# Attention with a position bias and a feed-forward layer: the mixed tile's scores, and the first unit's, straight from fp32 q and k

## The chip, the cores and the metric

The kernel runs on one core of one Trainium2 chip. A core has TensorE (PE in the profile; PEld is its weight load), VectorE (DVE), ScalarE (ACT), GpSimd (POOL), and SyncE (SP), which here issues every DMA. The metric is the device time of one execution in microseconds (us), the median of three runs.

## The reference

The kernel computes attention with a learned bias that depends on the distance of two positions, and then a feed-forward layer on the attention's output:

```
scores = q @ k.T / sqrt(64)                       # q, k, v: (4, 8, 576, 64)
psi_rel, psi_i = log1p(|i - j|), log1p(max(i, 1))
h = relu((psi_rel / psi_i)[..., None] @ w1 + b1)  # 32 hidden
scores += (h @ w2) per head                       # 8 heads
attn = softmax(scores);  a = attn @ v             # -> x: (2304, 512)
g = max(0.01 * y, y) with y = x @ w_in            # (512, 2048)
out = g @ w_out                                   # (2048, 512)
```

All inputs and outputs are fp32.

## The kernel before

There are three stages.

**The bias.** `gen_tick(g)` runs 36 times. A tick takes 16 rows of the bias for all heads: four relu tiles r of the hidden layer are made by DVE (L116) or ACT (L114), as a plan by costs decided; PE multiplies them with w2 (L127, four products of 32 output rows); ACT evicts the result into a tile e (L134, L135); SP writes e to a scratch array scr in DRAM (L146). From scr, `load_bias` (L163 to L172) reads the biases back, in the form that the scores want, as tiles "0", "1", "M", "2" and "3"; their loads are issued at ticks 16, 24, 27, 34 and 37.

**The attention.** It runs in 16 units u; a unit is a pair of heads and one batch entry. A unit has nine tiles in the order A0 B0 A1 B1 M A2 B2 A3 B3. A tile is 128 rows of scores by 576 columns; A tiles belong to the first head, B tiles to the second, and the mixed tile M holds the last 64 rows of both. `step(n)` handles tile n: `qk_mm` (scores, PE, L234), the reduction with bias (DVE, L258), then the transposes of tile n-3 (PE, L300 and L318), which ACT copies into PT (L316), then, where a group of tiles is complete, the product with v (PE, L335: 10 fp32 products of 64 output rows, each of which the profile shows as two records), then the exponential (ACT, L266). The scores' PSUM tile ps_s has two buffers, so the scores of tile n+2 wait for DVE's reduction of tile n. All is issued in a fixed order, written out by the program; each engine and SP's queue go through theirs in order.

The scores are made from two-part numbers: `split_hi` casts raw q (L196) and raw k (L201) to fp32r on DVE, `split_lo` takes the remainder on POOL (q L208, k L211). The tile qs has the high part of q in partitions 0 to 63 and the low part in 64 to 127; ks1 has k's high part, ks2 its low part, each in both halves. A tile of scores is then four products with all 128 partitions (two halves of 288 columns, with ks1 and with ks2). Tile M has eight, since the rows of the two heads need different k: the second half of the products is added onto the first, and a zero block of qs (set at L65) keeps each head's rows out of the other's.

The table SPL says at which tile i of unit u the splits of unit u+1 are issued. Those of unit 0 stand in the bias stage: from tick 6 on, every second tick issues one of `sp_ops` (q's cast, two q subtractions, k's cast, two k subtractions). `load_unit(u)` (L176 to L182) brings raw q and k of a unit into one of two pairs of tiles raw_b, each twice, once per partition half; units 0 and 1 are loaded at the start, unit u+2 after step i = 0 of unit u. `gen.close()` frees the bias stage's tiles at n = 8.

**The feed-forward layer.** It follows the last unit, with its own loads and products (L452, L478 to L480); the change does not touch it.

Of the kernel before, what the change touches and what calls it, by code (L numbers as in the profile page):

```python
# [8 lines left out]
F32 = mybir.dt.float32  # L9
F32R = mybir.dt.float32r  # L10
# [4 lines left out]
B, H, S, D, HID = 4, 8, 576, 64, 32  # L15
DM, DFF = 512, 2048
NT = B * S
HP = H // 2
KC = DM // 128
MF = DFF // 128  # L20
HS = S // 2
S0 = 512 - HS
PIT = S + 32
KW = 2 * S + 64
EARLY = 7
KINDS = ["A0", "B0", "A1", "B1", "M", "A2", "B2", "A3", "B3"]
GEN = [16, 17] + list(range(16)) + [34, 35] + list(range(18, 26)) + list(range(33, 25, -1))
SPL = {0: [(0, "q")], 1: [(1, "q", 0)], 3: [(1, "q", 1)], 4: [(0, "k")], 5: [(1, "k", 0)], 7: [(1, "k", 1)]}
GEN_AT = [39] * 9
LAG = 3  # L30
BLK = 512
# [5 lines left out]
def attention_ffn(ctx: ExitStack, tc: tile.TileContext, qt, kt, vm, vt, wi, wo, cst, out):  # L37
    nc = tc.nc
# [5 lines left out]
    gp = gen.enter_context(tc.tile_pool(name="gen", bufs=1, side="right"))  # L44
    att = ExitStack()
    ap = att.enter_context(tc.tile_pool(name="att", bufs=1, reuse_waits="tile"))
# [4 lines left out]
    def pstile(tag):  # L51
        shape = [128, 1024] if tag == "s" else [128, 512]
        return ps.tile(shape, F32, tag=tag, name="ps_" + tag)

    tmp_x = {(m, i): xp.tile([128, DM], F32, name=f"y{m}{i}") for m in range(5, EARLY) for i in range(2)}
    raw_b = [[ap.tile([128, c], F32, name=f"raw{c}{i}") for c in (2 * S, KW)] for i in range(2)]
# [3 lines left out]
    for t in vt_b:  # L60
        nc.vector.memset(t[0:64, 1, :], 0.0)
        nc.vector.memset(t[64:128, 0, :], 0.0)
    qs_b = [ap.tile([128, 1280], F32R, name=f"qs{i}") for i in range(2)]
    for t in qs_b:
        nc.vector.memset(t[:].rearrange("p (a c) -> p a c", a=2)[:, :, 576:640].bitcast(F32), 0.0)  # L65

    PT = ap.tile([128, 2, 10, HS], F32, name="PT")

    cs = gp.tile([128, S + 214], F32, name="cs")
    bps = gp.tile([128, 144], F32, name="bps")  # L70
    warm = gp.tile([128, 1], F32, name="warm")
# [19 lines left out]
    def gen_w(T):  # L91
        return max(S - 16 * T, 16 * T + 16)

    plan, load = [], {"a": 0.0, "v": 5.0}
    for T in GEN:
        w = gen_w(T)
# [77 lines left out]
    raw, qk, vv = {}, {}, {}  # L174

    def load_unit(u):  # L176
        hp, b = divmod(u, B)
        q_, k_ = raw_b[u % 2]
        for p in (0, 64):
            nc.sync.dma_start(out=q_[p:p + 64], in_=qt[hp, b])  # L180
            nc.sync.dma_start(out=k_[p:p + 64], in_=kt[hp, b])
        raw[u] = (q_, k_)  # L182

    def load_v(u):
# [7 lines left out]
    def split_hi(u, what):  # L192
        q_, k_ = raw[u]
        if what == "q":
            qs = qs_b[u % 2]
            nc.vector.tensor_copy(qs[:].rearrange("p (a c) -> p a c", a=2)[:, :, 0:S], q_[:].rearrange("p (a c) -> p a c", a=2))  # L196
            ks1 = ap.tile([128, KW], F32R, tag="ks1", name="ks1", bufs=2)
            ks2 = ap.tile([128, KW], F32R, tag="ks2", name="ks2", bufs=2)
            qk[u] = (qs, ks1, ks2)
        else:  # L200
            nc.vector.tensor_copy(qk[u][1][:], k_[:])  # L201

    def split_lo(u, what, a):
        q_, k_ = raw[u]
        qs, ks1, ks2 = qk[u]
        if what == "q":
            dst = qs[64:128, 640 * a:640 * a + S]
            nc.gpsimd.tensor_sub(dst, q_[64:128, S * a:S * a + S], dst.bitcast(F32))  # L208
        else:
            c = slice(S * a, KW if a else S)  # L210
            nc.gpsimd.tensor_sub(ks2[:, c], k_[:, c], ks1[:, c].bitcast(F32))  # L211

    st, pp = {}, {}

    def tile_id(n):
        u, i = divmod(n, 9)
        return u, KINDS[i]

    def qk_mm(n):
        u, kind = tile_id(n)  # L220
        qs, ks1, ks2 = qk[u]
        s_ = pstile("s")
        if kind == "M":
            prs = [(512, 0), (576, S + 64)]
        elif kind[0] == "A":
            prs = [(128 * int(kind[1]), 0)]
        else:
            prs = [(704 + 128 * int(kind[1]), S)]
        nmm = len(prs) * 2
        j = 0  # L230
        for c0, k0 in prs:
            for ks in (ks1, ks2):
                for hh in range(2):
                    nc.tensor.matmul(s_[:, S0 + HS * hh:S0 + HS * hh + HS], qs[:, c0:c0 + 128], ks[:, k0 + HS * hh:k0 + HS * hh + HS], start=(j == 0), stop=(j == nmm - 1))  # L234
                j += 1
        st[n] = s_

    mx_t, sm_t, rb_t, pair = {}, {}, {}, [None]
# [1 line left out]
    def softmax_a(n):  # L240
        u, kind = tile_id(n)
        hp = u // B
        bt = bias[hp, "M"][:] if kind == "M" else bias[hp, kind[1]][:, 0 if kind[0] == "A" else 1, :]
        col = 1 if kind[0] == "B" else 0
        if col == 0:
            mx_t[n] = ap.tile([128, 2], F32, tag="mx", name="mx", bufs=6)
        else:
            mx_t[n] = mx_t[n - 1]
        g, sc = int(KINDS.index(kind) > 4), 4 if kind == "M" else 2 * (int(kind[1]) % 2) + col
        if kind in ("A0", "A2"):  # L250
            sm_t[u, g] = ap.tile([128, 12], F32, tag="sm", name="sm", bufs=3)
        if kind == "M":
            pair[0] = ap.tile([128, S + 64], F32, tag="pM", name="pM", bufs=1)
        elif col == 0:
            pair[0] = ap.tile([128, 2 * S], F32, tag="p", name="p", bufs=3)
        p = pair[0][:, S * col:S * col + S]
        s_, i = st.pop(n), mx_t[n][:, col:col + 1]
        nc.vector.tensor_tensor_reduce(out=p, in0=s_[:, S0:S0 + S], in1=bt, scale=-0.125, scalar=3.4e38, op0=ALU.add, op1=ALU.min, accum_out=i)  # L258
        pp[n] = pair[0]
        ex_q.append((p, i, sm_t[u, g][:, sc:sc + 1]))  # L260
# [101 lines left out]
    def step(n):  # L362
        if n < NTILE:
            qk_mm(n)
            softmax_a(n)
        if 0 <= n - 1 < NTILE and KINDS[(n - 1) % 9] in ("M", "B3"):
            recip(n - 1)
        x_steps()
        while pv_out:
            pv_exit()  # L370
        if 0 <= n - LAG < NTILE:
            transposes(n - LAG, n + 2)
        if pv_q and pv_q[0][0] <= n:
            pv()
        while ex_q:
            softmax_b()
# [113 lines left out]
    with tc.manual_schedule():  # L490
        gen_setup()
        for u in range(2):
            load_unit(u)
            load_v(u)
        sp_ops = [(u, w, a) for u in range(1) for w, a in (("q", None), ("q", 0), ("q", 1), ("k", None), ("k", 0), ("k", 1))]
        done = -1
        early_ops = []
        for n in range(NTILE + LAG + 6):
            u, i = divmod(n, 9)
            if u == 0:  # L500
                while done < GEN_AT[i]:
                    gen_tick(done)
                    done += 1
                    if done >= 6 and done % 2 == 0 and sp_ops:
                        w = sp_ops.pop(0)
                        split_hi(*w[:2]) if w[2] is None else split_lo(*w)
            if n == 8:
                gen.close()
                early = ctx.enter_context(tc.tile_pool(name="early", bufs=1, side="right"))
                x_alloc(early, 0)  # L510
                w_alloc(early, 0)
                early.tile([128, 24], F32, name="gap")
                stage, stage_y = ExitStack(), ExitStack()
                pools["s"] = stage.enter_context(tc.tile_pool(name="stage", bufs=1, side="right"))
                pools["y"] = stage_y.enter_context(tc.tile_pool(name="stage_y", bufs=1, side="right"))
            step(n)
            if n == 13:
                w_fill()
                for m in range(EARLY):
                    early_ops += [(w_abs, m, h) for h in range(2)]  # L520
                    early_ops += [(w_bits, m, h, k) for k in range(4) for h in range(2)]
                    if m == 0:
                        early_ops += [(w_hi, 0, h) for h in range(2)] + [(w_lo, 0, h, nc.vector) for h in range(2)]
            for _ in range({0: 3, 4: 3}.get(i, 0) if n >= 18 else 0):
                if early_ops:
                    f, *args = early_ops.pop(0)
                    f(*args)
            if n == NTILE + 2:
                ffn1(0, 0)
            if u < HP * B:  # L530
                if u % B == B - 1 and u // B + 1 < HP:
                    c = {1: "0", 2: "1", 3: "M", 4: "2", 6: "3"}.get(i)
                    if c:
                        load_bias(u // B + 1, c)
                if u + 1 < HP * B:
                    for f, *args in SPL.get(i, ()):
                        (split_hi, split_lo)[f](u + 1, *args)
                if i == 0 and u + 2 < HP * B:
                    load_unit(u + 2)
                if i == 8 and u + 2 < HP * B:  # L540
                    load_v(u + 2)
        att.close()
# [35 lines left out]
        for j in range(len(seq) + 2):  # L578
            if j < len(seq):
                n, m = seq[j]  # L580
# [57 lines left out]
```

## Time and profile before

| | |
|---|---|
| three runs | 714.15, 712.75, 712.86 us; median 712.86 |
| the profiled execution | 713.1 us, its span 711.3 us |
| granted TensorE clock, mean | 0.999 |
| PE busy | 697.9 us, 98% of the span |
| DVE, ACT, POOL busy | 371.7, 362.6, 120.4 us |
| bias stage | from the start to about 56 us |
| attention | from about 56 us to about 315 us |
| feed-forward layer | from there to the end |

A row of the chain of waits gives the start, the time and the engine and line of one piece of the path that sets the end; a row of the timeline gives the records of one engine in order, with the idle time ahead of them in brackets. Records of products overlap (a weight load is done beside the product before it), so pieces of the chain, not record lengths, add up to time.

### The profile page before, as it was taken

How to read it: one execution, taken by the hardware profiler on the slowest of the kernel's cores; microseconds unless marked ns; L12 is line 12 of the kernel's file. 1: busy time of each engine (PE TensorE's matmuls, PEld its weight loads, DVE VectorE, ACT ScalarE, POOL GpSimd, SP SyncE). 2: the span in 40 equal slices, each digit the busy share in tenths (PEclk: the TensorE clock that was granted, in tenths of full speed). 3: DMA queues.
4: the chain of work that ended last, by engine and by line, in shares of the span. 5: the costliest groups of instructions: out<-in, count | busy, mean ns of one | idle time of the engine just before them, and what ended most of it. 6: DMA issues, size and time to landing. Idle time of an engine off the chain costs nothing.

```text
span 711.3 us, 11144 instructions
## 1 busy us (share of the span) xinstructions
PE 697.9 (98%) x4192; PEld 558.0 (78%) x4192; DVE 371.7 (52%) x876; ACT 362.6 (51%) x792; POOL 120.4 (17%) x143
## 2 busy tenths in 40 slices
PE   6899999999999999999999999999999999999997
PEld 2346888788888888877888888888888888888896
DVE  6996788878888878559995211122111221111111
ACT  7698778778787787684654221123111321222221
POOL 2203454445454444200000000000000000000000
PEclk9999999999999999999999999999999999999999
DMA  8798929755966772003550000001000010000100
GB/s 212 246 315 247 250 63 277 144 161 131 250 162 177 208 194 77 1 1 103 169 173 0 33 27 1 1 0 60 1 0 1 0 60 1 0 1 0 60 1 30
DMA packets 30262, 68.26 MB, mean 96 GB/s; under 512 B 8192, under 2 KB 8320, under 8 KB 30208
## 3 DMA queue, kind: packets, MB, share of 16 engines
q1 hardware_dynamic: 30208, 67.54, 33.7%
q8 instruction: 33, 0.54, 0.3%
q14 instruction: 21, 0.17, 0.1%
HBM read 51.92 MB, written 15.61 MB: 95 GB/s over the span
## 4 chain that ended last, share of the span: by engine, by line
PE 94%; DVE 3%; DMA 1%; issue 0%; ACT 0%; DVEq 0%; SPq 0%
PE ps_o L452 13%; PE ps_t L452 13%; PE ps_s L234 12%; PE ps_o L335 12%; PE ps_s L480 9%; PE ps_s L478 9%; PE ps_s L479 9%; PE ps_t L300 8%; PE ps_o L127 2%; PE ps_t L127 2%; DVE r L116 2%; PE ps_s L127 1%; PE ps_o L318 1%; PE ps_o L289 1%; DMA scr<-x 1%
## 5 line engine op out<-in xcount | busy, mean ns | idle before, releaser
L467 DVE TENSOR_TENSOR gl<-g,gh 128x512 fp32r<-128x512 f32 (+1 forms) x80 | 51.0, 638 | 266.2 <-ACT g L461 266.2
L234 PE MATMUL ps_s<-ks,qs 128*128 128x288 f32 x640 | 120.6, 315 | 1.5 <-DVE mx L258 1.5
L480 PE MATMUL ps_s<-woh,gl 128*128 128x512 f32 x288 | 112.1, 389 | 0.3 <-DVE gl L467 0.3
L478 PE MATMUL ps_s<-woh,gh 128*128 128x512 f32 x288 | 112.3, 390 | 0.0
L479 PE MATMUL ps_s<-wol,gh 128*128 128x512 f32 x288 | 112.2, 390 | 0.0
L258 DVE CUSTOM_DVE_ANT_0 p<-ps_s,bias 128x576 f32<-128x576 f32 x128 | 94.2, 750 | 26.0 <-PE ps_s L234 24.1
L234 PEld LDWEIGHTS ps_s<-ks,qs 128*128 128x128 f32 x640 | 89.7, 189 | 16.1 <-issue 8.2
L266 ACT ACTIVATE p<-p,mx 128x576 f32<-128x576 f32 x128 | 100.0, 781 | 3.7 <-DVE mx L258 3.0
L316 ACT COPY PT<-ps_t 128x512 f32<-128x512 f32 x128 | 73.9, 578 | 53.6 <-PE ps_t L300 53.6
L460 ACT ACTIVATE gh<-ps_o 128x512 fp32r<-128x512 f32 (+1 forms) x39 | 21.5, 552 | 126.6 <-PE ps_o L452 126.6
L460 ACT ACTIVATE gh<-ps_t 128x512 fp32r<-128x512 f32 (+1 forms) x39 | 21.5, 552 | 112.0 <-PE ps_t L452 111.9
L300 PE MATMUL ps_t<-ident,p 128*128 128x128 f32 x512 | 76.4, 272 | 0.0
L335 PE MATMUL ps_o<-PT,v 128*64 128x288 f32 x512 | 69.2, 412 | 0.0
L480 PEld LDWEIGHTS ps_s<-woh,gl 128*128 128x128 f32 x288 | 54.1, 188 | 12.1 <-DVE gl L467 0.7
L300 PEld LDWEIGHTS ps_t<-ident,p 128*128 128x128 f32 x512 | 62.4, 140 | 0.4 <-issue 0.4
L479 PEld LDWEIGHTS ps_s<-wol,gh 128*128 128x128 f32 x288 | 54.1, 188 | 10.7
L478 PEld LDWEIGHTS ps_s<-woh,gh 128*128 128x128 f32 x288 | 54.1, 188 | 10.6
L452 PE MATMUL ps_t<-xh,wil 128*128 128x512 f32 (+1 forms) x156 | 57.3, 367 | 0.0
L452 PE MATMUL ps_o<-xh,wil 128*128 128x512 f32 (+1 forms) x156 | 57.3, 367 | 0.0
L452 PE MATMUL ps_o<-xl,wih 128*128 128x512 f32 (+1 forms) x156 | 57.3, 367 | 0.0
L452 PE MATMUL ps_t<-xl,wih 128*128 128x512 f32 (+1 forms) x156 | 57.3, 367 | 0.0
L452 PE MATMUL ps_o<-xh,wih 128*128 128x512 f32 (+1 forms) x156 | 57.2, 367 | 0.0
(108 smaller groups left out, 1075.6 us busy)
## 6 DMA issues: line engine op xcount, KB each, us to landing
raw<-kt SPq DMA_DIRECT2D x32, 304.0 KB, 6.0
raw<-qt SPq DMA_DIRECT2D x32, 288.0 KB, 5.8
raw<-wi SPq DMA_DIRECT2D x16, 512.0 KB, 4.1
raw<-wo SPq DMA_DIRECT2D x16, 512.0 KB, 3.6
scr<-x SPq DMA_DIRECT2D x21, 295.5 KB, 4.2
bias<-scr SPq DMA_DIRECT2D x16, 288.0 KB, 5.4
out<-x SPq DMA_DIRECT2D x18, 256.0 KB, 2.1
v<-vm SPq DMA_DIRECT2D x16, 256.0 KB, 5.2
```

The lines of the kernel that those rows point to most:

```text
L234: nc.tensor.matmul(s_[:, S0 + HS * hh:S0 + HS * hh + HS], qs[:, c0:c0 + 128], ks[:, k0 + HS * hh:k0 + HS * hh + HS], start=(j == 0), stop= ...
L258: nc.vector.tensor_tensor_reduce(out=p, in0=s_[:, S0:S0 + S], in1=bt, scale=-0.125, scalar=3.4e38, op0=ALU.add, op1=ALU.min, accum_out=i)
L266: nc.scalar.activation(out=p, in_=p, func=AF.Exp, bias=i, scale=-1.0, accum_out=sm)
L300: nc.tensor.transpose(t0[:, 128 * jb:128 * jb + 128], p[:, p0 + 128 * jb:p0 + 128 * jb + 128], ident[:])
L316: nc.scalar.copy(out=PT[:, g, 0:8, c].rearrange("p (j h) c -> p j h c", h=2)[:, :, h, :], in_=t0[:].rearrange("p (j c) -> p j c", j=4))
L335: nc.tensor.matmul(o[64 * h:64 * h + 64, 0:HS], l, r, start=(jb == 0), stop=(jb == 4))
L452: nc.tensor.matmul(h_[:, :N], w, x[:, :N], start=(j == 0), stop=(j == len(mms) - 1))
L460: nc.scalar.activation(out=gh[:, :N], in_=h_[:, :N], func=AF.Prelu, alpha=0.01)
L467: nc.vector.tensor_sub(gl[:, :N], g[:, :N], gh[:, :N].bitcast(F32))
L478: nc.tensor.matmul(o, gh[:, c], wt[m][2][:], start=(m == 0), stop=False)
L479: nc.tensor.matmul(o, gh[:, c], wt[m][3][:], start=False, stop=False)
L480: nc.tensor.matmul(o, gl[:, c], wt[m][2][:], start=False, stop=(m == MF - 1))
```

## The change

Three things are done.

1. Tile M's scores are four fp32 products of one quadrant each: raw q and k of one partition half hh (partitions 64 hh to 64 hh + 63) give 288 columns of scores, in a PSUM bank of their own; head h goes to output rows 64 h to 64 h + 63. No part is added to another, so the zero blocks of qs and their memsets are gone, and qs has 1024 columns in place of 1280. Its cast is 1024 columns wide (1152 before), and each q subtraction 512 (576).
2. In unit 0 every tile reads raw fp32 q and k: two products per tile, one per partition half, each of 64 contracted rows and 288 columns. Unit 0 has no casts and no subtractions. Its raw tiles are its own (raw_0), in the bias stage's pool, which is now closed at n = 9.
3. Since tile M reads raw q and k, `load_unit(u+2)`, which overwrites them, is issued behind M's scores (i = 4), not after step i = 0; a unit's four raw loads go q, q, k, k. The q cast moves from i = 0 to i = 1 and q's first subtraction from i = 1 to i = 2; k's splits stay.

```diff
--- before.py
+++ after.py
@@ -25,7 +25,7 @@
 EARLY = 7
 KINDS = ["A0", "B0", "A1", "B1", "M", "A2", "B2", "A3", "B3"]
 GEN = [16, 17] + list(range(16)) + [34, 35] + list(range(18, 26)) + list(range(33, 25, -1))
-SPL = {0: [(0, "q")], 1: [(1, "q", 0)], 3: [(1, "q", 1)], 4: [(0, "k")], 5: [(1, "k", 0)], 7: [(1, "k", 1)]}
+SPL = {1: [(0, "q")], 2: [(1, "q", 0)], 3: [(1, "q", 1)], 4: [(0, "k")], 5: [(1, "k", 0)], 7: [(1, "k", 1)]}
 GEN_AT = [39] * 9
 LAG = 3
 BLK = 512
@@ -60,12 +60,11 @@
     for t in vt_b:
         nc.vector.memset(t[0:64, 1, :], 0.0)
         nc.vector.memset(t[64:128, 0, :], 0.0)
-    qs_b = [ap.tile([128, 1280], F32R, name=f"qs{i}") for i in range(2)]
-    for t in qs_b:
-        nc.vector.memset(t[:].rearrange("p (a c) -> p a c", a=2)[:, :, 576:640].bitcast(F32), 0.0)
+    qs_b = [ap.tile([128, 1024], F32R, name=f"qs{i}") for i in range(2)]
 
     PT = ap.tile([128, 2, 10, HS], F32, name="PT")
 
+    raw_0 = [gp.tile([128, c], F32, name=f"raw{c}") for c in (2 * S, KW)]
     cs = gp.tile([128, S + 214], F32, name="cs")
     bps = gp.tile([128, 144], F32, name="bps")
     warm = gp.tile([128, 1], F32, name="warm")
@@ -175,10 +174,10 @@
 
     def load_unit(u):
         hp, b = divmod(u, B)
-        q_, k_ = raw_b[u % 2]
-        for p in (0, 64):
-            nc.sync.dma_start(out=q_[p:p + 64], in_=qt[hp, b])
-            nc.sync.dma_start(out=k_[p:p + 64], in_=kt[hp, b])
+        q_, k_ = raw_b[u % 2] if u else raw_0
+        for t, src in ((q_, qt), (k_, kt)):
+            for p in (0, 64):
+                nc.sync.dma_start(out=t[p:p + 64], in_=src[hp, b])
         raw[u] = (q_, k_)
 
     def load_v(u):
@@ -193,7 +192,7 @@
         q_, k_ = raw[u]
         if what == "q":
             qs = qs_b[u % 2]
-            nc.vector.tensor_copy(qs[:].rearrange("p (a c) -> p a c", a=2)[:, :, 0:S], q_[:].rearrange("p (a c) -> p a c", a=2))
+            nc.vector.tensor_copy(qs[:].rearrange("p (a c) -> p a c", a=2), q_[:].rearrange("p (a c) -> p a c", a=2)[:, :, 64:S])
             ks1 = ap.tile([128, KW], F32R, tag="ks1", name="ks1", bufs=2)
             ks2 = ap.tile([128, KW], F32R, tag="ks2", name="ks2", bufs=2)
             qk[u] = (qs, ks1, ks2)
@@ -204,8 +203,8 @@
         q_, k_ = raw[u]
         qs, ks1, ks2 = qk[u]
         if what == "q":
-            dst = qs[64:128, 640 * a:640 * a + S]
-            nc.gpsimd.tensor_sub(dst, q_[64:128, S * a:S * a + S], dst.bitcast(F32))
+            dst = qs[64:128, 512 * a:512 * a + 512]
+            nc.gpsimd.tensor_sub(dst, q_[64:128, S * a + 64:S * a + S], dst.bitcast(F32))
         else:
             c = slice(S * a, KW if a else S)
             nc.gpsimd.tensor_sub(ks2[:, c], k_[:, c], ks1[:, c].bitcast(F32))
@@ -218,21 +217,29 @@
 
     def qk_mm(n):
         u, kind = tile_id(n)
+        s_ = pstile("s")
+        q_, k_ = raw[u]
+        if kind == "M":
+            for hh in range(2):
+                r = slice(64 * hh, 64 * hh + 64)
+                for h in range(2):
+                    k0 = (S + 64) * h + HS * hh
+                    nc.tensor.matmul(s_[64 * h:64 * h + 64, S0 + HS * hh:S0 + HS * hh + HS], q_[r, S * h:S * h + 64], k_[r, k0:k0 + HS], start=True, stop=True)
+            st[n] = s_
+            return
+        c0, k0, h = 128 * int(kind[1]), 0, 0
+        if kind[0] == "B":
+            c0, k0, h = c0 + 512, S, 1
+        if u == 0:
+            for hh in range(2):
+                r, c = slice(64 * hh, 64 * hh + 64), c0 + 64 + 64 * h
+                nc.tensor.matmul(s_[:, S0 + HS * hh:S0 + HS * hh + HS], q_[r, c:c + 128], k_[r, k0 + HS * hh:k0 + HS * hh + HS], start=True, stop=True)
+            st[n] = s_
+            return
         qs, ks1, ks2 = qk[u]
-        s_ = pstile("s")
-        if kind == "M":
-            prs = [(512, 0), (576, S + 64)]
-        elif kind[0] == "A":
-            prs = [(128 * int(kind[1]), 0)]
-        else:
-            prs = [(704 + 128 * int(kind[1]), S)]
-        nmm = len(prs) * 2
-        j = 0
-        for c0, k0 in prs:
-            for ks in (ks1, ks2):
-                for hh in range(2):
-                    nc.tensor.matmul(s_[:, S0 + HS * hh:S0 + HS * hh + HS], qs[:, c0:c0 + 128], ks[:, k0 + HS * hh:k0 + HS * hh + HS], start=(j == 0), stop=(j == nmm - 1))
-                j += 1
+        for j, ks in enumerate((ks1, ks2)):
+            for hh in range(2):
+                nc.tensor.matmul(s_[:, S0 + HS * hh:S0 + HS * hh + HS], qs[:, c0:c0 + 128], ks[:, k0 + HS * hh:k0 + HS * hh + HS], start=(j == 0), stop=(j == 1))
         st[n] = s_
 
     mx_t, sm_t, rb_t, pair = {}, {}, {}, [None]
@@ -362,6 +369,8 @@
     def step(n):
         if n < NTILE:
             qk_mm(n)
+            if n % 9 == 4 and n // 9 + 2 < HP * B:
+                load_unit(n // 9 + 2)
             softmax_a(n)
         if 0 <= n - 1 < NTILE and KINDS[(n - 1) % 9] in ("M", "B3"):
             recip(n - 1)
@@ -492,7 +501,6 @@
         for u in range(2):
             load_unit(u)
             load_v(u)
-        sp_ops = [(u, w, a) for u in range(1) for w, a in (("q", None), ("q", 0), ("q", 1), ("k", None), ("k", 0), ("k", 1))]
         done = -1
         early_ops = []
         for n in range(NTILE + LAG + 6):
@@ -501,10 +509,7 @@
                 while done < GEN_AT[i]:
                     gen_tick(done)
                     done += 1
-                    if done >= 6 and done % 2 == 0 and sp_ops:
-                        w = sp_ops.pop(0)
-                        split_hi(*w[:2]) if w[2] is None else split_lo(*w)
-            if n == 8:
+            if n == 9:
                 gen.close()
                 early = ctx.enter_context(tc.tile_pool(name="early", bufs=1, side="right"))
                 x_alloc(early, 0)
@@ -535,8 +540,6 @@
                 if u + 1 < HP * B:
                     for f, *args in SPL.get(i, ()):
                         (split_hi, split_lo)[f](u + 1, *args)
-                if i == 0 and u + 2 < HP * B:
-                    load_unit(u + 2)
                 if i == 8 and u + 2 < HP * B:
                     load_v(u + 2)
         att.close()
@@ -604,7 +607,8 @@
     perm = np.r_[0:256, 288:544, 256:288, 544:576]
     q, k, v = inputs["q"], inputs["k"], inputs["v"]
     qd = q.transpose(1, 0, 3, 2)[:, :, :, perm]
-    qd = np.concatenate([qd[0::2, :, :, None, :], np.concatenate([qd[1::2, :, :, 512:], qd[1::2, :, :, :512]], -1)[:, :, :, None, :]], 3)
+    qd = np.concatenate([qd[:, :, :, 512:], qd[:, :, :, :512]], -1)
+    qd = np.stack([qd[0::2], qd[1::2]], 3)
     kd = k.transpose(1, 0, 3, 2)
     kd = np.concatenate([kd[0::2], kd[1::2, :, :, 512:], kd[1::2]], -1)
     vd = v.transpose(1, 0, 2, 3).reshape(HP, 2, B, S, D).transpose(0, 2, 3, 1, 4).reshape(HP, B, S, 2 * D)
```

What moves on PE at the start of the attention: first the program before, from the fourth tile of unit 0 (the first two rows) over the transposes of its first tile and tile M to its sixth tile (ks_259 and ks_260 are k's parts, qs_100 is q's, p the tile of exponentials):

```order
L234 MATMUL ps_s<-ks_259,qs_100 128x288 x2
L234 MATMUL ps_s<-ks_260,qs_100 128x288 x2
L300 MATMUL ps_t<-ident,p 128x128 x4
L234 MATMUL ps_s<-ks_259,qs_100 128x288 x2
L234 MATMUL ps_s<-ks_260,qs_100 128x288 x2
L234 MATMUL ps_s<-ks_259,qs_100 128x288 x2
L234 MATMUL ps_s<-ks_260,qs_100 128x288 x2
L300 MATMUL ps_t<-ident,p 128x128 x4
L318 MATMUL ps_o<-ident,p 128x128
L234 MATMUL ps_s<-ks_259,qs_100 128x288 x2
```

And the program after, from the last product of the bias stage (raw_103 is q's raw tile, raw_104 k's):

```order
L126 MATMUL ps_t<-r,cs 32x432 x4
L236 MATMUL ps_s<-raw_104,raw_103 128x288 x8
L307 MATMUL ps_t<-ident,p 128x128 x4
L227 MATMUL ps_s<-raw_104,raw_103 64x288 x4
L307 MATMUL ps_t<-ident,p 128x128 x4
L325 MATMUL ps_o<-ident,p 128x128
L236 MATMUL ps_s<-raw_104,raw_103 128x288 x2
L307 MATMUL ps_t<-ident,p 128x128 x4
L236 MATMUL ps_s<-raw_104,raw_103 128x288 x2
```

The four tiles ahead of the first transposes are eight products in place of sixteen, tile M is four in place of eight (and of another shape, 64 output rows), and every later tile of the unit is two in place of four, each between transposes.

On PE around tile M of unit 1, before (the M products stand between two rows of transposes; the row with 64x288 x8 is the product with v):

```order
L300 MATMUL ps_t<-ident,p 128x128 x4
L234 MATMUL ps_s<-ks_787,qs_101 128x288 x2
L234 MATMUL ps_s<-ks_788,qs_101 128x288 x2
L234 MATMUL ps_s<-ks_787,qs_101 128x288 x2
L234 MATMUL ps_s<-ks_788,qs_101 128x288 x2
L300 MATMUL ps_t<-ident,p 128x128 x4
L318 MATMUL ps_o<-ident,p 128x128
L335 MATMUL ps_o<-PT,v 64x288 x8
L335 MATMUL ps_o<-PT,vt_91 64x288 x2
```

After:

```order
L307 MATMUL ps_t<-ident,p 128x128 x4
L227 MATMUL ps_s<-raw_85,raw_84 64x288 x4
L307 MATMUL ps_t<-ident,p 128x128 x4
L325 MATMUL ps_o<-ident,p 128x128
L342 MATMUL ps_o<-PT,v 64x288 x8
L342 MATMUL ps_o<-PT,vt_91 64x288 x2
L242 MATMUL ps_s<-ks_782,qs_101 128x288 x2
```

Tile M's products are now one row of raw k and q; what stands ahead of and behind them is the same.

On DVE in the bias stage, before:

```order
L116 TENSOR_SCALAR r<-cs,bps 128x512 x3
L196 CAST qs_100<-raw_82 128x2x576
L116 TENSOR_SCALAR r<-cs,bps 128x496 x3
L116 TENSOR_SCALAR r<-cs,bps 128x480 x3
L116 TENSOR_SCALAR r<-cs,bps 128x464 x4
L116 TENSOR_SCALAR r<-cs,bps 128x448 x3
L116 TENSOR_SCALAR r<-cs,bps 128x432 x3
L116 TENSOR_SCALAR r<-cs,bps 128x416 x4
L201 CAST ks_259<-raw_83 128x1216
L116 TENSOR_SCALAR r<-cs,bps 128x400 x3
L116 TENSOR_SCALAR r<-cs,bps 128x384 x4
L116 TENSOR_SCALAR r<-cs,bps 128x368 x3
```

After:

```order
L115 TENSOR_SCALAR r<-cs,bps 128x512 x3
L115 TENSOR_SCALAR r<-cs,bps 128x496 x3
L115 TENSOR_SCALAR r<-cs,bps 128x480 x3
L115 TENSOR_SCALAR r<-cs,bps 128x464 x4
L115 TENSOR_SCALAR r<-cs,bps 128x448 x3
L115 TENSOR_SCALAR r<-cs,bps 128x432 x3
L115 TENSOR_SCALAR r<-cs,bps 128x416 x4
L115 TENSOR_SCALAR r<-cs,bps 128x400 x3
L115 TENSOR_SCALAR r<-cs,bps 128x384 x4
L115 TENSOR_SCALAR r<-cs,bps 128x368 x3
```

The two casts are gone and the r tiles follow one another; nothing else moves there.

## Rows read from the trace of the kernel before

**Rows 1.** The page: busy time by engine; the chain's shares by engine.
```profile
PE 697.9 (98%) x4192; PEld 558.0 (78%) x4192; DVE 371.7 (52%) x876; ACT 362.6 (51%) x792; POOL 120.4 (17%) x143
...
PE 94%; DVE 3%; DMA 1%; issue 0%; ACT 0%; DVEq 0%; SPq 0%
```

**Rows 2.** Chain of waits, 150 to 170 us: start us, us, what.
```profile
154.13 1.06 PE ps_s L234 x8
155.19 0.44 PE ps_t L300 x4
...
155.73 2.58 PE ps_o L335 x20
...
159.47 0.53 PE ps_s L234 x4
...
166.56 0.73 PE ps_s L234 x4
```

**Rows 3.** Timeline of PE, three short windows: start us, us, what, count.
```profile
155.66 0.46 PE L335 MATMUL ps_o<-PT,v 128*64 128x288 f32 x2
...
156.20 0.41 PE L335 MATMUL ps_o<-PT,v 128*64 128x288 f32 x2
...
157.17 0.41 PE L335 MATMUL ps_o<-PT,v 128*64 128x288 f32 x2
```

**Rows 4.** Chain of waits, 14 to 31 us.
```profile
14.49 0.76 DVE qs L196
15.25 3.47 DVE r L116 x3
...
24.86 0.70 DVE ks L201
```

**Rows 5.** Groups of DVE's L116 by shape: busy us, mean ns of one.
```profile
L116 DVE TENSOR_SCALAR r<-cs,bps 128x496 f32<-128x496 f32 x6 | 4.8, 852 | 0.0
L116 DVE TENSOR_SCALAR r<-cs,bps 128x400 f32<-128x400 f32 x6 | 4.6, 820 | 0.0
...
L116 DVE TENSOR_SCALAR r<-cs,bps 128x416 f32<-128x416 f32 x7 | 2.6, 423 | 0.0
L116 DVE TENSOR_SCALAR r<-cs,bps 128x512 f32<-128x512 f32 x6 | 2.5, 481 | 0.0
```

**Rows 6.** Timeline of POOL, 10 to 32 us.
```profile
15.39 3.04 POOL L208 TENSOR_TENSOR qs<-raw,qs 64x576 fp32r<-64x576 f32 x2 [11.12 <-DVE qs L196]
25.70 3.08 POOL L211 TENSOR_TENSOR ks<-raw,ks 128x576 fp32r<-128x576 f32 x2 [7.27 <-issue]
```

**Rows 7.** Windows: length, busy PE, PEld, DVE, ACT, POOL, clock, DMA share, GB/s.
```profile
20.00:40.00 20.00, 18.51 (x134) 7.51 (x131) 20.00 (x52) 15.87 (x37) 3.08 (x2) 1.00 0.78 249
```

**Rows 8.** Chain of waits, 56 to 72 us.
```profile
56.30 0.74 PE ps_s L234 x4
...
58.86 4.44 DMA scr<-x
...
63.46 2.85 DMA bias<-scr
...
67.27 0.80 PE ps_s L234 x4
```

**Rows 9.** Windows up to the last write of the bias, columns as in rows 7.
```profile
23.00:63.30 40.30, 37.92 (x280) 18.38 (x274) 37.62 (x98) 34.42 (x81) 5.91 (x4) 1.00 0.84 266
30.00:32.00 2.00, 2.00 (x18) 0.94 (x16) 2.00 (x7) 1.61 (x4) 0.00 (x0) 1.00 0.00 0
35.00:62.00 27.00, 26.12 (x205) 13.22 (x197) 24.32 (x68) 24.44 (x57) 2.83 (x2) 1.00 0.96 308
```

**Rows 10.** Waits in 0 to 75 us: total us, times, longest.
```profile
PE ps_s L234 <- DVE mx L258: 1.5, 3, 0.6
```

**Rows 11.** Timeline of DVE, 103.4 to 108 us: tile M's reduction and the idle time ahead.
```profile
107.71 0.76 DVE L258 CUSTOM_DVE_ANT_0 pM<-ps_s,biasM 128x576 f32<-128x576 f32 x1 [0.47 <-PE ps_s L234]
```

**Rows 12.** The page's DMA issues: count, KB each, median us to landing.
```profile
raw<-qt SPq DMA_DIRECT2D x32, 288.0 KB, 5.8
```

## The prediction

> **What bounds the kernel now.** I read the page first: PE is busy 98% of the span and carries 94% of the chain, so time is PE's own pieces, and what does not reach PE's path is free; DVE, ACT and POOL have slack over the whole span [rows 1]. Then, since a share is a mean over three stages, the windows and the chain stage by stage. In the attention, 150 to 170 us, the chain is PE's alone: tile M's eight score products are a piece of 1.06 us, a normal tile's four 0.53, four transposes 0.44, a product with v 2.58 [rows 2]. The bias stage differs: DVE is busy for all 20.00 us from 20 to 40 [rows 7], and the casts of unit 0 and the r tiles behind them are pieces of the chain [rows 4]. At the end of that stage the chain leaves the engines: the last bias rows take 4.44 us to scr and 2.85 back, and PE's score piece at 67.27 is the first that waits for them [rows 8]. The feed-forward stage is not touched; it starts earlier by what the first two give.
>
> **Part 1: tile M in fp32 quadrants, units 1 to 15.** Its price goes by the product with v, the fp32 product that the trace has. In that row 20 records take 2.58 us [rows 2]; two records run in pairs, and the pairs at 156.20 and 157.17 are four rounds apart, so a round is 0.97 / 4 = 0.243 us [rows 3]. Ten rounds are 2.43; the other 0.15 is paid on entry. Behind it a score piece takes 0.73 in place of 0.53 [rows 2], 0.20 on leaving. So a visit to the half-array fp32 products costs 0.155 + 0.20 = 0.355. Tile M is four products of two records each, eight records; if the four quadrants run side by side as the two column halves do, that is two rounds, 0.485 + 0.355 = 0.84, 0.22 below 1.06, and fifteen times that is **3.3 us**. The bounds: nothing shows a visit cheaper than 0.20, which with two rounds makes 0.69 (5.6 in all); two rounds turning into four make 1.325 (4.0 lost, a rival below); at 1.06 nothing is won. I take 0.84, since rounds and visit are both read from the neighbouring product. The Trainium skill speaks for a little less: "TensorE: Matmul & The Clock Gate", Part 3 "Measured speedup vs the span model", gives four packed row tiles 3.07 times the speed of one after another, not 4; by it the eight records would take 8 x 0.243 / 3.07 = 0.63 for 0.485 and the sum would be 2.2 us higher, an estimate by that page, and no run here shows it. Unit 0's tile M lies in the stretch of part 2.
>
> **Part 2: unit 0 without splits.** Removed from DVE are casts of 0.76 and 0.70 us on the chain [rows 4]; start to start of the next instruction they are about 1.4. The second loss is larger: three r operations behind each cast take 3.47 [rows 4], 852 and 820 ns each by shape where wider and narrower ones take 481 (512 columns) and 423 (416) [rows 5]. The two slow shapes stand where POOL's subtractions run, 15.39 to 18.43 and 25.70 to 28.78 [rows 6]. Between the neighbours I take 0.47 for 496 columns and 0.415 for 400: 6 x 0.38 + 6 x 0.405 = 4.7. With the subtractions gone DVE ends 1.4 + 4.7 = **6.1 us** earlier, and since DVE has no idle time there [rows 7], PE and ACT, which wait for it, do too.
>
> What is late next is the last bias. Its write waits for the queue of transfers: from 23 to 63.3 us 266 GB/s were moved, 40.3 x 266 = 10.7 MB; the full stretch 35 to 62 shows 308 GB/s at 0.96 share, and 30 to 32 nothing at all [rows 9]. The 10.7 MB at 308 GB/s need 34.7 us, 5.6 less. So of 6.1 the end of the last write can come forward **5.6**; if only the empty 2 us are recovered it is 2.0; more than 6.1 has no source. I take 5.6, because the stretch at 308 GB/s is also the longest and the tiles that feed it come evenly once DVE is not held up.
>
> That gain holds if PE has unit 0 ready. Before, unit 0 starts at 56.30 and PE is ready for the waiting piece 0.6 before 67.27 [rows 8, 10], 10.35 us later. After, the first four tiles are one stretch of fp32 products, whose waits for DVE (0.9 us beside the 0.6) [rows 10] absorb the difference of 4 x 0.485 + 0.355 to 4 x 0.53; tile M saves 0.22; the four tiles behind it stand between transposes and cost 0.84 each for 0.53, 1.25 in all. So 11.4 us from a start at 50.2: ready at 61.6, against the bias at 67.27 - 5.6 = 61.7. It just fits; an error of half a microsecond here costs as much, and is in the range.
>
> **Part 3: what is moved.** The q cast stands one reduction later, two reductions ahead of tile M's; tile M's reduction had 0.47 us of idle time in front of it in a unit with much other DVE work [rows 11], and the cast is 0.7 us. Where it comes late, the buffer for the tile two further on comes late; a normal tile and its transposes (0.53 + 0.44) [rows 2] cover most. I take 0.02 per unit, **0.3 us**; nothing as the lower bound, 0.1 per unit (1.5) as the upper. The raw loads are issued behind tile M's scores, at 155.2 for the M of 154.13, and read by a cast behind the second tile of the next unit, at about 167.3 (behind the piece at 166.56) [rows 2]: 12 us against 5.8 to landing [rows 12]. On SP they stand ahead of what step i = 4 to 8 issues there, the v loads above all, and those are asked for a unit later. That is free with double the time in hand; if the cover went, PE would stop at the next unit's first tile for the excess.
>
> Costed at nothing: shorter casts and subtractions (under PE's pieces in the attention), the two memsets (under the first load), the later close of the bias pool (tiles that nothing reads before the feed-forward stage is prepared).
>
> **Sum**, in the profiled execution's 713.1 us (span 711.3): 713.1 - 3.3 - 5.6 + 0.3 = 704.5. The median of the runs, 712.86, lies 0.24 below the profiled one, so **704.3 us**.
>
> **The rivals.** (a) *Row halves take turns.* No row of before has two products that differ in partition half; all pairs of [rows 3] are column halves over 128 rows. If the two partition halves run one after the other, tile M is four rounds, 1.325 us, 15 x 0.265 = 4.0 lost; unit 0 grows by two rounds for each of nine tiles, 4.4, of which 0.9 is absorbed: ready at 65.1, and only 2.2 of the bias gain is left. 713.1 + 4.0 - 2.2 + 0.3 - 0.2 = 715.0, slower. It decides from an M piece of about 1.2 us on. For it: no row shows the case; against: two column halves share the array at no loss [rows 3].
> (b) *Order in the passes.* If products start strictly in the order given, with both records of one ahead of the next, four quadrants take five rounds: 1.57 for tile M, 7.6 lost, with 3.7 left of the bias gain: 717. Against it, the first two records of the product with v start together, and pairs from the first on [rows 3]. The Trainium skill, "TensorE: Matmul & The Clock Gate", Part 3 "The mechanism", has products start and end in program order; its rows agree on order, but show no first record of one product beside the second of another, which this rival would ask for.
> (c) *The transfers keep most of part 2.* The writes of the bias go out in small pieces, and each needs its e tile back; if only the empty stretch is recovered, 2.0 in place of 5.6: 707.9.
> (d) *The quadrants change nothing.* If changing to quarter-array products costs 0.22 more than to half-array ones, tile M stays at 1.06 and part 1 is nothing: 707.6.
> (e) *DVE becomes the bound around tile M.* With the cast 0.75 late in every unit, not covered, 15 x 0.6 = 9 eats all the gains: 713 to 714. Against it the idle time in [rows 11].
>
> **How the numbers follow.** The forecast has 0.60, (a) 0.11, (b) 0.03, (c) 0.14, (d) 0.08, (e) 0.04. The forecast's own range goes from 701.2 (tile M at 0.69, all 6.1 of part 2, 0.24 for the runs) to 707. The range that should hold 8 in 10 reaches over (c) and (d) with part 3 at its upper bound, 713.1 - 2.0 - 3.3 + 1.5 = 709.3, and a little on either side: **700.8 to 710.5**. A measurement of this kernel tells 0.2%, 1.4 us, from no change. Forecast, (c) and (d) are faster by more, together 0.82, of which 0.02 goes to mixtures of (c) and (d); (a) and (b) are slower, 0.14, and with a part of (e) 0.15; the rest, 0.05, is within.
>
> **What would show it.** Part 1: tile M's piece in the chain, 0.84; 1.3 says (a), 1.57 (b), 1.06 (d). Part 2: the r operations of 496 and 400 columns at 0.47 and 0.42 in the mean; the first score of unit 0 at 50.2, the write of the last bias ending at 57.7, the waiting piece of unit 1 at 61.7; if that piece waits for PE and not for the transfer, unit 0's fp32 tiles are dearer than I made them. Part 3: PE's waits for DVE in the attention stay under 0.1 us a unit, and no cast waits for a raw tile. The forecast is wrong if tile M's piece does not shorten, or if the bias loads end less than 4 us earlier.

## The result, and the profile after

The changed kernel takes 703.26 us (median of four runs, 702.97 to 703.62) against 713.08 (four runs); the ratio is 0.9864, interval 0.9849 to 0.9878. The forecast was 704.3. The profiled execution's span is 701.2, 10.1 less than before. PE is still the chain (its shares by engine):

```profile
PE 95%; DMA 1%; ACT 1%; DVE 1%; issue 0%; SPq 0%; DVEq 0%
```

Tile M, in the chain of waits from 140 to 165 us (start, us, what), answers to [rows 2]:

```profile
146.02 0.43 PE ps_t L307 x4
146.46 0.65 PE ps_s L227 x8
147.10 0.58 PE ps_t L307 x4
...
162.06 0.65 PE ps_s L227 x8
```

Its piece went from 1.06 to 0.65, but the transposes behind it from 0.44 to 0.58: what tile M pays on leaving stands in the next row. Together 1.23 for 1.50, 0.27 less. From one tile M to the next it is 15.60 us (146.46 to 162.06); before, 15.87, from the tile M at 154.13 [rows 2] to the next in the chain before:

```profile
170.00 1.06 PE ps_s L234 x8
```

The end of the bias stage, chain of waits from 49 to 63 us, answers to [rows 8]:

```profile
49.98 0.74 PE ps_s L236 x4
...
52.76 4.00 DMA scr<-x
...
56.91 2.86 DMA bias<-scr
...
60.73 0.79 PE ps_s L242 x4
```

The attention starts 6.32 us earlier (56.30 to 49.98). PE's score piece that waits for the last bias, called the waiting piece below, is 6.54 earlier (67.27 to 60.73). DVE's r operations by shape (busy us, mean ns) show why; they answer to [rows 5]:

```profile
L115 DVE TENSOR_SCALAR r<-cs,bps 128x496 f32<-128x496 f32 x6 | 2.5, 476 | 0.0
...
L115 DVE TENSOR_SCALAR r<-cs,bps 128x400 f32<-128x400 f32 x6 | 2.2, 425 | 0.0
```

And the windows (length, busy PE, PEld, DVE, ACT, POOL, clock, DMA share, GB/s), which answer to [rows 7, 9]: the empty two microseconds are gone. The third ends where the last write of the bias lands (52.76 + 4.00).

```profile
0.00:23.00 23.00, 18.17 (x143) 8.45 (x144) 17.45 (x52) 20.26 (x43) 1.28 (x7) 1.00 0.94 267
20.00:40.00 20.00, 20.00 (x158) 8.65 (x154) 20.00 (x60) 18.92 (x45) 0.00 (x0) 1.00 0.98 326
23.00:56.76 33.76, 33.35 (x256) 14.80 (x253) 31.87 (x89) 31.31 (x74) 2.51 (x2) 1.00 0.94 306
30.00:32.00 2.00, 2.00 (x25) 1.09 (x24) 2.00 (x8) 1.22 (x3) 0.00 (x0) 1.00 0.96 328
```

The first of them before:

```profile
0.00:23.00 23.00, 16.92 (x122) 7.08 (x124) 17.49 (x45) 17.28 (x36) 4.32 (x9) 1.00 0.93 250
```

The account: 6.54 from the bias stage, 15 x 0.265 = 3.98 from tile M, and 0.34 and 0.1 lost in two units (below): 10.1, as in the span.

### The profile page after: what moved, and what is told of

Read it like the earlier page. It is cut to its first block, busy times and chain, and to the rows that moved or that the text cites. A ratio compares the mean times of both kernels' runs of the same rounds, so it can differ in the third digit from the quotient of the medians.

```text
span 701.2 us, 11179 instructions
## 1 busy us (share of the span) xinstructions
PE 691.4 (99%) x4192; PEld 542.1 (77%) x4192; DVE 368.2 (53%) x872; ACT 362.9 (52%) x792; POOL 109.9 (16%) x139
## 4 chain that ended last, share of the span: by engine, by line
PE 95%; DMA 1%; ACT 1%; DVE 1%; issue 0%; SPq 0%; DVEq 0%
PE ps_o L461 14%; PE ps_t L461 13%; PE ps_o L342 12%; PE ps_s L242 10%; PE ps_s L489 9%; PE ps_s L488 9%; PE ps_s L487 9%; PE ps_t L307 9%; PE ps_o L126 2%; PE ps_t L126 2%; PE ps_s L227 1%; PE ps_s L126 1%; PE ps_o L296 1%; PE ps_o L325 1%; ACT r L113 1%; DMA scr<-x 1%
## 5 line engine op out<-in xcount | busy, mean ns | idle before, releaser
L242 PE MATMUL ps_s<-ks,qs 128*128 128x288 f32 x480 | 93.7, 317 | 0.2 <-DVE mx L265 0.2
L242 PEld LDWEIGHTS ps_s<-ks,qs 128*128 128x128 f32 x480 | 67.6, 189 | 13.6 <-issue 6.1
L487 PEld LDWEIGHTS ps_s<-woh,gh 128*128 128x128 f32 x288 | 54.1, 188 | 10.7
```

What stands on the lines that cost most here:

```text
L487: nc.tensor.matmul(o, gh[:, c], wt[m][2][:], start=(m == 0), stop=False)
```

## The experiments

The runs were made in three sets, each with its own runs of the kernel before. These took 712.99 us in the set of the quadrants alone, the first version of unit 0 alone, the one half, and tile M beside the product with v in all units; 712.71 in the set of the second version of unit 0 alone, POOL's subtractions, the casts and the q cast at i = 0; 713.37 (eight runs) in the set of the mixed casts and the last two. The edits are shown shortened, with ... for what is left out.

**The quadrants alone.** Unit 0's other tiles get their splits in the bias stage again.

```diff
-        if u == 0:
+        if False:
+        sp_ops = [(u, w, a) for u in range(1) for w, a in (("q", None), ...)]
...
+                        split_hi(*w[:2]) if w[2] is None else split_lo(*w)
```

> Tile M in fp32 quadrants in all units, with the moved raw loads and the moved q cast, but unit 0's other tiles from splits in the bias stage as before. Theory (the two gains are separate and add up): only tile M's share is seen, 15 x 0.27 us less what one moved cast costs, 0.3: 3.7 below the kernel before, about 709.4, with unit 0 starting at 56.3 as before. Rival (nearly all of the gain is the bias stage's, and a shorter tile M is given back by later waits): no change, 713. Rival (the raw loads' later place helped the bias transfers): the first piece that waits for the bias ends earlier than 67.2 here too.

708.75 us, ratio 0.9939 (0.9925 to 0.9954): 4.24 less than before, where 3.7 was expected. Tile M's piece is 0.65. The rest lies in the bias stage, as the last rival had it, but 0.8 of it is an earlier start of the attention and not faster transfers:

```profile
55.52 0.74 PE ps_s L242 x4
...
66.36 0.80 PE ps_s L242 x4
```

The attention starts 0.8 earlier and the waiting piece 0.9, with the splits still there. Of the 0.8, 0.45 is there before the first cast (14.04 for 14.49 us), in part because the first load took 2.65 us for 2.87, which differs from run to run (2.60 to 2.87). Only the other 0.3 can come from the narrower cast and subtractions (POOL's pair 2.78 for 3.04). The memsets that are gone had ended at 2.1, with DVE idle behind them until that load landed at 3.59.

**Unit 0 alone.** A first version kept unit 0 in the shared raw tiles.

```diff
+        if u == 0:
+            q_, k_ = raw[0]
...
+            st[n] = s_
+            return
...
-        sp_ops = [(u, w, a) for u in range(1) ...]
+        sp_ops = []
```

> The kernel before with unit 0 alone from fp32 q and k (its tile M too); every other unit, loads and casts as before. Theory: the bias stage ends 6.3 us earlier and the piece that waits for the last bias 6.5 earlier, so 6.5 below the kernel before, about 706.6; tile M of units 1 to 15 stays at 1.06. Rival (the transfers of the bias only follow with the raw loads' new order and tiles): the wait ends 2 to 4 us earlier, 709 to 711.

725.52 us, and a faulty edit: the load for unit 2 is issued behind step 0, so from the second tile on unit 0 read unit 2's q and k, and PE waited for them, a piece of 6.80 us of the raw load on the chain. So this run says nothing of the theory, but it shows why the change needs raw tiles of its own for unit 0. The second version has them:

```diff
+    raw_0 = [gp.tile([128, c], F32, name=f"raw{c}") for c in (2 * S, KW)]
...
-        q_, k_ = raw_b[u % 2]
+        q_, k_ = raw_b[u % 2] if u else raw_0
```

> The kernel before with unit 0 alone from fp32 q and k, now from raw tiles of its own, which no later load overwrites; every other unit, the order of loads and the casts as before. Theory (the shares add up; from the quadrants alone, 708.75, to the whole change, 703.26, unit 0 was worth 5.5): 5.5 to 6.3 below the kernel before, 706.7 to 707.5, tile M of units 1 to 15 at 1.06. Rival (unit 0's gain is there only with the other loads' order): 709 to 711.

707.13 us, ratio 0.9916 (0.9899 to 0.9934): 5.6 less, with tile M of units 1 to 15 at 1.06. With the 4.2 of the quadrants alone that is 9.8, the whole change's 9.8 (713.08 to 703.26). The times add up within their intervals. The pieces do so less exactly: the waiting piece moved by 0.91 and by 6.04 (to 61.23) in the two, by 6.54 in the whole, so there the two shares are not independent.

**One partition half for all of tile M.**

```diff
-                r = slice(64 * hh, 64 * hh + 64)
+                r = slice(0, 64)
```

> The changed kernel with all four products of tile M reading the same partition half (0 to 63), in place of one half for each half of the columns; the results are the same. Theory (the two partition halves run side by side, and this is what makes tile M two rounds): four rounds, tile M's piece 0.65 + 0.485 = 1.13, 15 x 0.485 = 7.3 above the changed kernel, 710.5. Rival (the partition halves bring nothing, and the quadrants only gain from the column halves): no change, 703.3.

710.07 us, 6.8 above the changed kernel. Chain of waits, 140 to 165 us:

```profile
148.92 1.12 PE ps_s L227 x8
150.04 0.59 PE ps_t L307 x4
```

The piece grew by 0.47, close to two rounds of 0.243. So partition halves run side by side and rival (a), the halves taking turns, is out.

**POOL's subtractions back.** The copies of two columns only release them.

```diff
+                        if w % 3 == 0:
+                            nc.vector.tensor_copy(busy[w // 3][:]...[:, :, 0:1], q_[:]...[:, :, 0:1])
+                        else:
...
+                            nc.gpsimd.tensor_sub(busy[w // 3][p, c], (q_, k_)[w // 3][p, c], (q_, k_)[w // 3][p, c])
```

> The changed kernel with four subtractions put back on POOL in the bias stage, of the sizes and at the places of those removed (64 x 576 twice, 128 x 576 twice), released by DVE copies of two columns; nobody reads their results. Theory (POOL's subtractions stretch DVE's r operations beside them): the shapes of 496 and 400 columns are at about 0.85 and 0.82 again, the attention starts 4.7 later, and the time is 4.5 to 5 above the changed kernel, 708. Rival (the r operations were slow for what stood ahead of them on DVE, the casts): no change, 703.3. Rival (the bias transfers set the end, and DVE's time is half hidden): r operations slow, time up by 2.

706.98 us, 3.7 above the changed kernel. DVE's shapes and POOL's timeline:

```profile
L115 DVE TENSOR_SCALAR r<-cs,bps 128x496 f32<-128x496 f32 x6 | 4.3, 766 | 0.0
L115 DVE TENSOR_SCALAR r<-cs,bps 128x400 f32<-128x400 f32 x6 | 4.0, 714 | 0.0
```

```profile
14.71 2.52 POOL L522 TENSOR_TENSOR busy<-raw 64x576 f32<-64x576 f32 x2 [10.52 <-DMA raw<-kt]
23.87 2.43 POOL L522 TENSOR_TENSOR busy<-raw 128x576 f32<-128x576 f32 x2 [6.64 <-issue]
```

The same two shapes are slow again, with no cast ahead of them. These subtractions are shorter than the real ones (4.95 us for 6.12), and so is what DVE loses: the 12 operations lose 3.5 us here and 4.7 in the kernel before, 0.70 us and 0.77 us per microsecond of POOL. The attention starts at 53.82, 3.84 later, the waiting piece at 65.14, 4.41 later (in the profiled execution, which took 707.40 for 702.97). The delay is not half hidden by transfers.

**The casts back, without the subtractions.**

```diff
+                        if w == 0:
+                            nc.vector.tensor_copy(busy[:, 0:2 * S], q_[:])
+                        if w == 3:
+                            nc.vector.tensor_copy(busy[:], k_[:])
```

> The changed kernel with unit 0's two casts put back on DVE in the bias stage (1152 and 1216 columns, from fp32 to fp32r, into a tile that nobody reads), without the subtractions. Theory: DVE is later by the casts alone, 1.4, and so is the end, 704.7; the r operations stay at 0.48 and 0.43. Rival (the casts, not the subtractions, stretch the r operations): 4 to 6 later, 708. Rival (transfers set the end): no change.

704.15 us, 0.9 above the changed kernel; the attention starts at 51.21, 1.23 later, the waiting piece at 62.40, 1.67 later, and the r operations stay at 464 and 413 ns. So the casts cost their own length and stretch nothing.

**The q cast back at i = 0.**

```diff
-SPL = {1: [(0, "q")], 2: [(1, "q", 0)], 3: ...
+SPL = {0: [(0, "q")], 1: [(1, "q", 0)], 3: ...
```

> The changed kernel with the q cast and the first q subtraction of the next unit back at steps i = 0 and i = 1, as before the change. Theory (the move let one subtraction on POOL fall beside one wide operation of the weights' preparation on DVE, 1.74 for 0.69, and one unit grew by 0.34): all units at 15.6, 0.3 below the changed kernel, 702.9. Rival (the move is free or helps, because the raw load has more time): 703.3 or later.

702.77 us, ratio to before 0.9855 (0.9839 to 0.9870), for 0.9864 of the changed kernel: not told apart by time. The traces do tell two things. In the changed kernel one unit, from tile M at 130.51 to tile M at 146.46, takes 15.95 us and one 15.70; here none is above 15.64. There, the chain's piece and the timelines of DVE and POOL:

```profile
130.51 0.65 PE ps_s L227 x8
```

```profile
132.13 1.74 DVE L431 SCALAR_TENSOR_TENSOR tmp<-raw,tmp 128x512 int32<-128x512 int32 x1
...
257.72 2.36 DVE L431 SCALAR_TENSOR_TENSOR y<-raw,y 128x512 int32<-128x512 int32 x2
```

```profile
132.05 1.27 POOL L207 TENSOR_TENSOR qs<-raw,qs 64x512 fp32r<-64x512 f32 x1
...
257.60 1.33 POOL L207 TENSOR_TENSOR qs<-raw,qs 64x512 fp32r<-64x512 f32 x1
```

The moved subtraction fell on DVE's wide operation on the weights, mean 0.70 in the kernel with the casts at i = 0; in the second place one of the two operations took 1.76. The runs of the quadrants alone, of POOL's subtractions and of the casts, which keep the move, have the long unit too (15.95, 15.98, 15.97). Against that, in unit 0 the cast at i = 0 goes ahead of a reduction (chain of waits, 49 to 63 us):

```profile
51.51 0.08 DVE mx L265
51.59 0.60 DVE qs L195
52.19 0.32 DVE p L265
...
61.30 0.80 PE ps_s L242 x4
```

and the waiting piece is 0.57 later.

**Casts at i = 0 in units 1 to 14, at i = 1 in unit 0.**

```diff
+SPL1 = {**SPL, 0: [(0, "q")], 1: [(1, "q", 0)], 2: []}
-                    for f, *args in SPL.get(i, ()):
+                    for f, *args in (SPL if u == 0 else SPL1).get(i, ()):
```

> The changed kernel with the q cast and first q subtraction back at steps i = 0 and 1 in units 1 to 14, and at i = 1 and 2 only in unit 0, where DVE's cast would stand ahead of the reductions that PE waits for. Theory (moving the cast cost 0.34 in one unit and gained 0.5 at the end of unit 0, so both together cancelled in the kernel with the cast moved back everywhere): 0.3 below the changed kernel, 702.9, with all units at 15.6 and the first piece that waits for the last bias at 60.7. Rival (the two numbers are run to run scatter): 703.3, the piece anywhere from 60.7 to 61.3.

702.40 us, ratio 0.9849 (0.9836 to 0.9862). By time this is not told apart from the changed kernel's 0.9864 (0.9849 to 0.9878). In the trace the waiting piece stands at 60.63 and every unit takes 15.60 to 15.65: both halves of the account.

**Tile M beside the product with v**, in all units ahead of it.

```diff
-        if n < NTILE:
+        if n < NTILE and n % 9 != 4:
             qk_mm(n)
...
             transposes(n - LAG, n + 2)
+        if n < NTILE and n % 9 == 4:
+            qk_mm(n)
+            ... load_unit(n // 9 + 2)
+            softmax_a(n)
```

> The changed kernel with tile M's scores issued behind the transposes of that step, directly ahead of the product with v. Theory (a visit costs on entry and on leaving, because the shape of the products changes, and two visits side by side cost once): what tile M pays on leaving (0.14) and the product with v on entry (0.15) falls away in 15 units, 4.4 us, 698.9. Rival (the change from quarter-array to half-array products costs as much as any other): 703.3, no change. Rival (tile M's reduction, 0.55 us later, makes PE wait for the buffer of the scores): slower than 703.3, with waits of PE for DVE behind the product with v.

702.33 us, 0.9 below the changed kernel, where 4.4 were expected. Chain of waits, 140 to 165 us:

```profile
146.39 0.87 PE ps_t L307 x8
...
147.38 0.65 PE ps_s L227 x8
148.02 2.58 PE ps_o L342 x20
150.60 0.73 PE ps_s L242 x4
```

The transposes are at 0.87 for eight, so tile M's leaving cost is gone; but the product with v is at 2.58 still. The entry cost, 0.15 of the 2.58, is paid again from quarters to halves of the array. The Trainium skill, "TensorEngine Tiling (Array Packing)", "Key Properties", says that a change of tiling mode drains TensorE; this row agrees in so far as the 0.15 us are there, but shows no drain as such. A unit takes 15.46 where nothing else intervenes, 0.15 less. In four units the eight transposes in one row take 1.07 to 1.08, and the waiting piece is 0.55 later, with tile M later in unit 0 as well: 15 x 0.15 - 4 x 0.2 - 0.55 is the 0.9.

**The same in units 1 to 15 only, with the mixed casts.**

```diff
+        late = 9 < n < NTILE and n % 9 == 4
+        if n < NTILE and not late:
             qk_mm(n)
...
             transposes(n - LAG, n + 2)
+        if late:
+            qk_mm(n)
...
+            softmax_a(n)
```

> As the kernel with mixed casts, and tile M's scores directly ahead of the product with v in units 1 to 15 (unit 0 as changed). Theory (side by side saves what tile M paid on leaving, 0.14, and no more; in four units the eight transposes in one row wait 0.2 for ACT's copy): 702.9 - 15 x 0.15 + 4 x 0.2 = 701.4. Rival (the 0.55 that the first unit lost there had another cause): 702.

701.15 us (700.96 to 702.02), ratio 0.9833 (0.9820 to 0.9846): the fastest of all, 1.25 below the mixed casts in the same set, where 1.5 was expected; the waiting piece stands at 60.55. So the 0.55 of unit 0 did come from tile M's place there.

**And behind the product with v.**

```diff
             pv()
+        if late:
+            qk_mm(n)
...
+            softmax_a(n)
```

> The same with tile M's scores behind the product with v. Theory (a visit is paid on entry and on leaving whatever its shape, tile M's entry stays, the product with v leaves into tile M at no cost): 0.14 less per unit as well, 701.4. Rival (tile M's reduction is 3.2 us later and DVE has it and the next tile's at once, so PE waits for a buffer of the scores in each unit): 15 times 0.3 or more, 706 or later.

731.47 us, ratio 1.0257 (1.0234 to 1.0281). Chain of waits, 140 to 165 us, and the row of PE's timeline in which it ends:

```profile
160.26 0.72 PE ps_s L228 x8
...
161.11 0.76 DVE pM L266
...
162.88 0.70 DVE ks L201
163.59 0.67 DVE p L266
```

```profile
164.32 0.80 PE L243 MATMUL ps_s<-ks,qs 128*128 128x288 f32 x4 [1.04 <-DVE mx L266]
```

The chain goes from PE to DVE and back: tile M's reduction comes late, the weights' operations and k's cast stand ahead of the next reduction, and PE, which has two more tiles and their transposes to do meanwhile, then stands still for 1.04 us. It is the rival of the expectation, but at about 1.9 us a unit above the kernel with mixed casts ((731.47 - 702.40) / 15) and not 0.3. PE's waits for DVE are 16.1 us in all, 13 of them, up to 2.0. A part of the rest is the clock, as a window shows (columns as above):

```profile
149.00:150.00 1.00, 1.00 (x7) 1.00 (x6) 0.77 (x2) 0.45 (x3) 1.00 (x1) 0.50 1.02 406
```

From 148 to 150 us the granted clock is 0.50, 1.2 GHz in place of 2.4, after PE had stood still for 1.84 us up to 145.68. Over the four stretches of 40 us from 140 to 300 us the clock is 0.96, 0.98, 0.98 and 0.96 in the mean, from which some 5 us can be estimated for it. The rest of the 29 us stays open.

## Why the prediction was right

**Part 1** was right in mechanism and low in size: 3.3 forecast, 3.98 measured. Rounds and entry came out (0.485 + 0.16 = 0.65); the term that was too dear is the leaving cost, taken from scores behind the product with v (0.20), which is 0.14 in front of transposes. The one-half run shows the two rounds themselves. By the figure 3.07 of the Trainium skill ("TensorE: Matmul & The Clock Gate", Part 3 "Measured speedup vs the span model"), which is for four row tiles, the piece would be 0.15 longer, an estimate; the trace does not agree: two partition halves at once save 0.47 of 0.485. Rivals (a), (b) and (d), with tile M at 1.325, 1.57 and 1.06, fall by the measured 0.65. Rival (e) falls by PE's waits for DVE's reductions: none between 62 and 290 us, and units of 15.60 but for the two of part 3.

**Part 2**, DVE: 6.1 forecast, 6.32 measured at the start of the attention. The split in 4.7 for the stretch and 1.4 for the casts is borne out by the two runs that put one of them back (3.84 at four fifths of POOL's work, and 1.23).

The term that was mis-sized is the cap by transfers: 10.7 MB at 308 GB/s were to hold the gain to 5.6, and the last write landed 6.54 earlier, at 56.76. The rate came out: from 23 us to that landing 306 GB/s were moved, and with unit 0 alone 309 (from 23 to 57.31). Over 20 us it can be more, 326 from 20 to 40, but these two do not show that the whole stretch could have gone faster than the 308 of the cap. The amount did not come out: 33.76 x 306 is 10.3 MB, not 10.7, because 0.4 MB more had been moved in the first 23 us (267 GB/s for 250), and the prediction kept the amount of the program before. What brought these 0.4 MB forward is open: with unit 0 alone the first 23 us have 255, and there the last write landed at 57.31, near the 57.7 that was forecast; with the casts back they have 272. The write was issued 6.10 earlier (58.86 to 52.76), about as much as the attention's start moved, and took 4.00 to land in place of 4.44; a delay of DVE came through whole (3.84 gave 4.41, and 1.23 gave 1.67). Rival (c) falls.

PE in unit 0 was to be ready 11.4 us after its start, at 61.6; it waits 0.17 before 60.73, so it was ready 10.6 after. The tiles behind tile M cost what was worked out, in other rows: a score piece of 0.69 and transposes of 0.59, 1.28, for 0.84 + 0.44 (read in the kernel with unit 0 alone). The stretch ahead of tile M came out shorter, with one wait of 0.41 for two of 0.33 and 0.56. That is part 3's moved cast: with the cast at i = 0 again the second wait is back (0.52) and PE is ready 11.2 after its start. The conclusion that it just fits stands, with 0.17 us of waiting, but by luck: bias and PE were both about a microsecond earlier than forecast.

**Part 3** was near in size, 0.34 and 0.1 for 0.3, by luck, for it was wrong in kind: not 0.02 in each unit, but a collision of POOL with DVE in two units. That the move also paid 0.5 at the end of unit 0 was not seen. The later raw loads cost nothing: no cast waits for one. Of what was costed at nothing, the memsets were worth nothing; the shorter splits can have gained 0.3 in the bias stage of the quadrants alone, but the whole change has no splits there.

## What to carry to other kernels

Where DVE is the bound, look at what POOL does beside it before counting DVE's own instructions: unit 0's subtractions, off every path, cost more than three times what its casts did. Products on halves and quarters of the array do run side by side, and their price is the change of shape on entering and leaving: read it in the pieces of the neighbours, not in their own. A cap worked out as an amount over a rate needs both for the program after: here the rate came out, and the amount, read from the program before, did not.

## What the runs showed of the hardware that was not expected

A subtraction on POOL stops some of DVE's operations nearly whole. The operation on the weights began 0.08 us behind POOL's start at 132.05 and ended at 133.87, 0.55 behind POOL's end at 133.32; its mean is 0.70 in the kernel with the casts at i = 0. The Trainium skill, "SBUF — State Buffer", "SBUF: two separate sides", has the two engines share a pair of ports as a lock and not by bandwidth; the trace agrees but for the 0.15 us that were done meanwhile. DVE's reduction of the scores, which reads one operand from PSUM, took 0.75 wholly beside POOL's work, as without it:

```profile
137.75 0.75 DVE L265 CUSTOM_DVE_ANT_0 p<-ps_s,bias 128x576 f32<-128x576 f32 x1
```

```profile
137.67 1.43 POOL L210 TENSOR_TENSOR ks<-raw,ks 128x576 fp32r<-128x576 f32 x1
```
